# Smaller first projections, a last unit in two halves, and paired port operations in a planned attention kernel

## The chip, the cores and the metric

The kernel runs on one core of a Trainium2 chip. The metric is the device time of one execution in microseconds; less is better. The engines are named as in the profile: PE multiplies matrices (PEld loads its weights), ACT evaluates functions, DVE and POOL work element by element, SP issues DMAs; ACT issues a few DMAs too.

## The reference

Two independent blocks work on inputs of 2048 rows by 512 columns in bf16, and their outputs stand side by side. A is a linear attention, B a full softmax attention, each with 32 heads of 16 columns:

```python
# A: phi(t) = where(t > 0, t + 1, exp(t)) + 1e-6
kv = einsum("bhsd,bhse->bhde", phi(k), v);  z = einsum("bhsd->bhd", phi(k))
o = einsum("bhqd,bhde->bhqe", phi(q), kv) / (einsum("bhqd,bhd->bhq", phi(q), z)[..., None] + 1e-6)
# B: softmax over 2048 keys for 32 heads of 16 columns
p = softmax(einsum("bhqd,bhkd->bhqk", q, k) * 0.25);  o = einsum("bhqk,bhkd->bhqd", p, v)
# each: out = o @ wo
```

## The kernel before, in words

**Work.** Nearly all the work is B's scores: 32 heads x 2048 x 2048. Heads are taken eight at a time (head group `Gp`, four of them), queries 512 at a time (chunk `c`), and even and odd heads apart (`e_`): 32 units `u`. In a unit, four heads lie in four strips of 32 rows of the PE array, `g` = 0 to 3. K^T is kept twice in `KM`, once with the odd heads' rows at zero and once with the even ones', so that a strip of 32 rows yields one head. A block is one head, 128 keys (`j`, 16 of them) and 512 queries: a unit has 64 blocks, the kernel 2048.

**Two ways for a block.** Its score matmul (`qk`, L863) takes 32 rows of `KM` and of `QT`.
- The ACT way: three or two blocks at a time go into the PSUM tiles `pS0` (three banks) and `pS1` (two banks), which alternate, and ACT writes exp of them to `PT` (L1032).
- The D way: the block goes into one of the two banks of `pD`. DVE turns it into 16-bit integers whose bits are nearly those of exp (L944, into `DI`), and POOL adds two constants to these (L968, two blocks at a time, two shifted copies). Three such copies, each with its own scaled V (`VV`), together approximate the exponential.

Then the values are multiplied (L1107), one matmul for an ACT block and three for a D block, 17 columns per head (16 and a column of ones for the denominator), four heads side by side in four column strips, into `pPV`.

**End of a unit** (`unit_done`, L1123 to L1147). DVE transposes `pPV` in 32x32 squares (L1127), takes the reciprocals (L1133), POOL multiplies by them (L1134; DVE does so in the last unit), and after the odd unit DVE transposes back into `ON` (L1139). At the end `pre_job` (L794) multiplies three of the four head blocks of the last 512 rows by `wo` once all scores have been issued, and `last_job` (L805) adds the fourth and copies the result out with DVE or ACT. A copy by DVE is stored by SP, one by ACT by ACT itself (L814).

**A beside it.** A's projections, phi and outputs are jobs of matmuls and DVE operations in the same `pD` banks. `phi_stages` (L687) is an exponential on ACT (L691), a clamp on DVE (L692) and a combination on DVE (L693); `v4_job` (L665) makes `VV` and its two scaled copies (L680). The list of A's jobs is spread over the run by due times between 60 us and `TEND` - 60.

**The order of everything** comes from a planner that runs when the program is built (the loop at L1290). It keeps a clock `T` per engine, candidate operations with ready times and priorities, planned durations (a matmul of 512 columns `MM` = 0.2155, a group of score matmuls `QK` = 0.22, a change of kind of PE work `PH` = 0.11), and picks the earliest, with the priority deciding among those within 0.03 us. `fill_act_cand` (L984) offers the next score group for ACT, `fill_d_cand` (L1040) and `d_pick` a block for D if a `pD` bank is free, DVE's and POOL's backlog is small and no A job is overdue. So the number of blocks on each way is a result of the plan. `POLICY` (L254) has one row of 19 parameters, with a random seed among them, for each 8 us of planned time; the last row serves all later ones. Each engine then runs its own list strictly in the planned order and waits on semaphores where data or buffers ask for it.

**PORT.** The DVE operations of L680, L692 and L693 carry a key `"PORT"`. The planner starts one only when POOL is free and keeps POOL free until it has ended, and the POOL operations read the same key, so the order among them is fixed by semaphores. In the plan a handover costs nothing:

```python
st = max(T[eng], c_[0], T["pool"] if c_[5] else 0.0)          # L1318
...
if c_ is not None and c_[5]:
    T["pool"] = max(T["pool"], st + dur)                       # L1364
```

**The head** (L1150 to L1173) is written by hand. PE runs 28 matmuls on an identity matrix, then transposes the first four tiles of 128 rows of B's x (L562), which DVE and ACT in turn copy to `xTb` (L555). Then PE makes K^T of head group 0 for the first 512 rows (L587, four matmuls of 512 columns into the last bank of `pS1`), DVE writes its even and its odd version (L600), PE makes Q^T (into `pD` bank 0), and ACT copies it (L1166). The planner's clocks start after this, at 10.3 (ACT at 11.2).

## Time and profile before

| | us |
|---|---|
| median of 10 runs | 706.12 (705.59 to 708.21) |
| the profiled execution | 708.2 |
| its span, first to last instruction | 706.4 |
| first exponential starts | 12.21 |
| last exponential ends | 696.23 |
| ACT busy in the span | 686.6 (97%) |
| PE, DVE, POOL busy in the span | 655.9, 560.0, 568.5 |

The span is divided in three: a head before the first exponential, the long middle, and a tail after the last. The profile shows for each group of instructions its line, engine, output and input with their shapes, the count, the busy time, the mean of one in ns, and the idle time of the engine just before them with what ended most of it. An arrow `<-PE pD L863` reads: the wait ended when PE's instruction of L863 on tile pD was done. The number of blocks on each way can be read from the score matmuls: L863 with output pS is counted once for each ACT block, with output pD once for each D block. The granted clock is shown as 9 (90% or more) in all 40 slices; whether PE runs at its full rate is read from the distance of its instructions.

### The profile page before, as it was taken

What the parts mean: (1) busy time and instruction counts of PE and PEld (TensorE: products, weight loads), DVE (VectorE), ACT (ScalarE), POOL (GpSimd) and SP (SyncE); (2) the same over time, 40 slices, a digit from 0 to 9 for tenths busy, and PEclk for the clock granted to TensorE, in tenths of its full rate; (3) what the DMA queues carried; (4) which work ended last, traced back from release to release, by engine and by line L of the source; (5) the groups of instructions that cost most, each with busy time, mean ns of one, the idle gap of its engine ahead of it and who ended that gap; (6) DMA issues with size and microseconds to landing.
All of it is one profiled execution on the core that took longest, in us unless ns stands there. A gap on an engine that the chain in (4) does not pass through costs nothing.

```text
span 706.4 us, 15708 instructions
## 1 busy us (share of the span) xinstructions
PE 655.9 (93%) x6657; PEld 222.0 (31%) x6710; DVE 560.0 (79%) x1000; ACT 686.6 (97%) x642; POOL 568.5 (80%) x343
## 2 busy tenths in 40 slices
PE   8999999999999999999999999999999999999985
PEld 4324443233333333322222233322222222222221
DVE  4778878788788888878888887888888788878772
ACT  4999999999999999999999999999999999999994
POOL 4577666777889887796999879998789988898983
PEclk9999999999999999999999999999999999999999
DMA  9900000000000000010010001000011000101001
GB/s 214 230 4 2 1 2 9 5 12 9 2 2 1 2 1 2 8 39 9 18 38 16 2 1 23 17 21 18 9 31 24 16 1 32 32 31 31 24 9 34
DMA packets 35789, 17.34 MB, mean 25 GB/s; under 512 B 26496, under 2 KB 35200, under 8 KB 35712
## 3 DMA queue, kind: packets, MB, share of 16 engines
q1 hardware_dynamic: 34624, 15.61, 9.3%
q8 instruction: 54, 0.88, 0.5%
q10 hardware_dynamic: 1088, 0.66, 0.3%
q14 instruction: 23, 0.19, 0.1%
HBM read 4.72 MB, written 4.19 MB: 13 GB/s over the span
## 4 chain that ended last, share of the span: by engine, by line
ACT 82%; PE 6%; POOL 6%; DVE 3%; issue 1%; POOLq 0%; DVEq 0%; ACTq 0%
ACT PT L1032 80%; POOL DI L968 6%; ACT EA L691 2%; PE pPV L1107 2%; PE pS L863 2%; DVE DI L944 1%; PE pD L587 1%; PE pD L863 0%; PE pD L1152 0%; DVE KNa L693 0%; PE pD L701 0%; DVE VV L680 0%; PE pS L562 0%; PE pS L587 0%; DVE GR L657 0%
## 5 line engine op out<-in xcount | busy, mean ns | idle before, releaser
L1032 ACT ACTIVATE PT<-pS 128x1536 f16<-128x1536 f32 x587 | 673.8, 1368 | 2.5 <-PE pD L863 1.2
L968 POOL TENSOR_TENSOR DI<-DI,SHC 128x1024 int32<-128x1024 int32 x291 | 544.0, 1888 | 117.5 <-DVE DI L944 52.5
L944 DVE TENSOR_SCALAR DI<-pD 128x512 int16<-128x512 f32 (+1 forms) x572 | 382.5, 692 | 70.3 <-PE pD L863 63.1
L863 PE MATMUL pS<-QT,KM 32*128 32x512 bf16 x1467 | 229.3, 385 | 23.4 <-ACT PT L1032 18.0
L1107 PE MATMUL pPV<-DI,VV 128*17 128x512 f16 x1743 | 243.6, 382 | 1.8 <-POOL DI L968 0.9
L1107 PE MATMUL pPV<-PT,VV 128*17 128x512 f16 x1467 | 241.2, 382 | 1.2 <-ACT PT L1032 1.0
L863 PE MATMUL pD<-QT,KM 32*128 32x512 bf16 x581 | 205.9, 385 | 3.9 <-DVE DI L944 2.7
L863 PEld LDWEIGHTS pS<-QT,KM 32*128 32x128 bf16 x1467 | 56.3, 91 | 221.8 <-ACT PT L1032 180.4
L1107 PEld LDWEIGHTS pPV<-DI,VV 128*17 128x17 bf16 x1743 | 51.4, 88 | 65.6 <-issue 48.0
L1107 PEld LDWEIGHTS pPV<-PT,VV 128*17 128x17 bf16 x1467 | 51.6, 88 | 63.3 <-issue 46.9
L863 PEld LDWEIGHTS pD<-QT,KM 32*128 32x128 bf16 x581 | 49.7, 91 | 49.1 <-DVE DI L944 27.7
L701 PE MATMUL pD<-Wa,xTa 128*128 128x128 bf16 x512 | 36.9, 220 | 0.6 <-DVE DI L944 0.2
L587 PE MATMUL pD<-xTb,Wb 128*128 128x512 bf16 x101 | 29.8, 390 | 4.2 <-issue 2.8
L701 PEld LDWEIGHTS pD<-Wa,xTa 128*128 128x128 bf16 x512 | 28.7, 98 | 13.1 <-DVE DI L944 6.8
L1127 DVE STREAM_TRANSPOSE OT<-pPV 128x512 f32<-128x512 f32 x32 | 22.7, 709 | 8.3 <-PE pPV L1107 8.3
L1134 POOL TENSOR_TENSOR OT<-OT,ZR 128x256 bf16<-128x256 f32 x31 | 19.2, 619 | 7.5 <-DVE KNa L692 3.6
L671 PE MATMUL pD<-Wb,xTb 128*128 128x128 bf16 x256 | 17.8, 220 | 1.0 <-DVE KM L600 0.6
L704 DVE CAST KNa<-pD 128x256 bf16<-128x256 f32 x32 | 13.4, 417 | 6.4 <-PE pD L701 6.1
L782 PE MATMUL pD<-WOa,ONT 128*128 128x512 bf16 x52 | 15.6, 383 | 1.7 <-issue 1.7
L728 PE MATMUL pD<-xTa,Wa 128*128 128x512 bf16 x52 | 15.1, 382 | 1.9 <-issue 1.4
L693 DVE SCALAR_TENSOR_TENSOR KNa<-EA,KNa 128x256 bf16<-128x256 bf16 x32 | 13.4, 420 | 4.1 <-POOL DI L968 3.5
L676 DVE CAST VV<-pD 128x512 bf16<-128x512 f32 x16 | 11.0, 688 | 6.8 <-PE pD L671 6.6
(98 smaller groups left out, 301.3 us busy)
## 6 DMA issues: line engine op xcount, KB each, us to landing
out_dram<-OB SPq DMA_DIRECT2D x16, 128.0 KB, 1.7
out_dram<-KNa SPq DMA_DIRECT2D x14, 128.0 KB, 1.7
Wa<-in_A_wqkv_dram SPq DMA_DIRECT2D x1, 1536.0 KB, 8.3
KM<-KR SPq DMA_DIRECT2D x96, 16.0 KB, 1.8
Wb<-in_B_wqkv_dram SPq DMA_DIRECT2D x2, 384.0 KB, 5.0
Wb<-in_B_wqkv_dram SPq DMA_DIRECT2D x1, 512.0 KB, 4.8
WOa<-in_A_wo_dram SPq DMA_DIRECT2D x1, 512.0 KB, 9.0
VNa<-in_B_wo_dram SPq DMA_DIRECT2D x1, 512.0 KB, 3.7
```

Of the source, the lines that this page charges most:

```text
L587: return e.matmul(f32v(bk), lhsT=Wb[:, cc, kind * 512 + Gp * 128:kind * 512 + Gp * 128 + 128], rhs=xTb[:, cc, sc * 512:(sc + 1) * 512], st ...
L671: return e.matmul(f32v(bk)[:, tl * 128:(tl + 1) * 128], lhsT=xTb[:, cc, t * 128:(t + 1) * 128], rhs=Wb[:, cc, 1024 + Gp * 128:1024 + Gp * ...
L701: return e.matmul(f32v(bk)[:, 128 * x:128 * x + 128], lhsT=xTa[:, cc, (t + i_) * 128:(t + i_ + 1) * 128], rhs=Wa[:, cc, c0:c0 + 128], star ...
L728: return e.matmul(f32v(bk), lhsT=Wa[:, cc, bq * 128:(bq + 1) * 128], rhs=xTa[:, cc, sc * 512:(sc + 1) * 512], start=(cc == 0), stop=(cc == 3))
L782: return e.matmul(f32v(bk), lhsT=src, rhs=WO[:, hb, :], start=(hb == 0), stop=(hb == 3))
L863: return e.matmul(dst, lhsT=KM[32 * g:32 * g + 32, Gp % 2, e_, j * 128:(j + 1) * 128], rhs=QT[32 * g:32 * g + 32, Gp % 2, c * 512:(c + 1) ...
L944: sch.add("dve", lambda e: e.tensor_scalar(DI[:, buf, 0, i * 512:(i + n) * 512], DB[:, bi * 512:(bi + n) * 512], ESC, EB, op0=ALU.mult, op ...
L968: sch.add("pool", lambda e: e.tensor_tensor(DI32[:, buf, 1:3, 0:w], DI32[:, buf, 0, 0:w].unsqueeze(1).broadcast_to([128, 2, w]), SHC32[:]. ...
L1032: sch.add("act", lambda e: e.activation(PT[:, row, c0:c0 + w], SCR[sl][:, 0:w], ACTF.Exp, scale=SC), reads=skeys(sl), writes=[("PT", row, ...
L1107: sch.add("pe", lambda e, g=g, vk=vk, c0=c0, P=P, first=first, last_=last_: e.matmul(PVb[32 * g:32 * g + 17, 0:512], lhsT=VV[:, Gp % 2, vk ...
L1127: sch.add("dve", lambda e: e.transpose(OT[:, 0, :], PVb[:, 0:512]), reads=[("PV", g) for g in range(4)], writes=[("OT", 0)])
L1134: (ml, 0.65 if ml == "pool" else 0.36, f_op(ml, lambda e: e.tensor_tensor(xn[:, :, 16 * e_:16 * e_ + 16], o[:, :, 0:16], zr.unsqueeze(2).b ...
```

## The change

1. **Head.** The first K^T and Q^T are made in halves of 256 columns. On PE the order is: transposes of tiles 0 and 1, K half 0, transposes of tiles 2 and 3, Q half 0, Q half 1, K half 1. DVE writes four masked K pieces of 256 columns instead of two of 512 and copies Q half 1; ACT copies Q half 0. Two K halves lie in the two banks of `pS1`, the Q halves in the two `pD` banks. New keys `KMb` and `QTb` guard the second halves. The planner's clocks start at 7.8 (DVE 8.9, POOL 8.6).
2. **Tail.** The last unit is normalised in two halves of 256 queries (`final_done`), all four steps of one half before the other, all on DVE. `last_job` needs only its half. Its copies are ACT, ACT, DVE, ACT for the four tiles, where they were DVE, ACT, DVE, ACT. Two of the four `pre_job`s may run as soon as no more D blocks are offered (fewer than 12 blocks left).
3. **Pairs.** The two operations L692 and L693 become one planned step, and so do the two L680 of a V job; the instructions stay.
4. **Planner.** A handover of the port is planned: 0.065 from a POOL operation to a PORT operation, 0.17 back. Score groups avoid the row strips of the group just issued; one that shares none may be planned beside it, one that shares one costs 0.09 more. The overflow flag's three matmuls and the denominators' sixteen become parts that other work can come between.
5. **Table.** Nearly all rows of `POLICY` are replaced; there are 86 instead of 87.

```diff
+        def both(*fs):
+            op = lambda bk: [f(bk) for f in fs][-1]
+            op.keys = fs[0].keys
+            return op
+        LKG, LKV = 0.065, 0.17
+        poolop = [False]
+        QQ = 0.09
+        lastq = [(), 0.0]
...
         def flag_job(**kw):
-                ("pe", 1.5, f_pe(mm, k3 + ["identf"])),
+                *halves(mm, k3 + ["identf"], n=3, parts=3, dur=0.45),
...
         def v4_job(t4, Gp, **kw):
-            for k_ in range(2):
-                st.append(("dve", 0.21, f_op("dve", lambda e, k_=k_: e.tensor_scalar(v[k_ + 1], v[0], VSCALE[k_], None, op0=ALU.mult),
-                                             [("VV", r, 0, t4), ("VV1", r)], [("VV", r, k_ + 1, t4), "PORT"])))
+            st.append(("dve", 0.42, both(*[
+                f_op("dve", lambda e, k_=k_: e.tensor_scalar(v[k_ + 1], v[0], VSCALE[k_], None, op0=ALU.mult),
+                     [("VV", r, 0, t4), ("VV1", r)], [("VV", r, k_ + 1, t4), "PORT"]) for k_ in range(2)])))
...
         def phi_stages(n, t_ap, keys):
-                ("dve", 0.067 + n * 0.00026, f_op("dve", lambda e: e.tensor_scalar(...), [], list(keys) + ["PORT"])),
-                ("dve", 0.067 + n * 0.00105, f_op("dve", lambda e: e.scalar_tensor_tensor(...), [("EA", q)], list(keys) + ["PORT"]))]
+                ("dve", 0.134 + n * 0.00131, both(
+                    f_op("dve", lambda e: e.tensor_scalar(...), [], list(keys) + ["PORT"]),
+                    f_op("dve", lambda e: e.scalar_tensor_tensor(...), [("EA", q)], list(keys) + ["PORT"])))]
...
         def take(bl, parts):
+                if u == NU - 1 and left[u] < DEND and "dclosed" not in tok:
+                    tok["dclosed"] = T["pe"]
+                    urgent2.extend(pre_job(tl, "dclosed") for tl in range(2))
...
-                        urgent2.extend(pre_job(tl) for tl in range(4))
+                        urgent2.extend(pre_job(tl, "lastfill") for tl in range(2, 4))
...
         def fill_act_cand():
-            ch = choose(u, n)
+            prev = lastq[0] if pmode[0] == "q" else ()
+            ch = choose(u, n, prev)
...
-            start = max(T["pe"], t0, afree[sl] + LAT, buffree.get(src, 0.0) - 0.5)
-            dur = QK
+            hit = any(g in prev for _, _, g in bl)
+            start = max(lastq[1] + 0.05 if prev and not hit else T["pe"], t0, afree[sl] + LAT, buffree.get(src, 0.0) - 0.5)
+            dur = max(0.03, start + QK - T["pe"]) if start < T["pe"] else QK + (QQ if hit else 0.0)
+            start = max(start, T["pe"])
...
         def fill_d_cand():
-            at = max(T["pe"], min(fr), busy - P["DLEAD"], T["pe"] + d_backlog(T["pe"]) - P["DBL"] + 0.01)
+            prev = tuple(lastq[0]) if pmode[0] == "q" else ()
+            early_ = len(prev) < 4 and bool(prev)
+            at = max(lastq[1] + 0.05 if early_ else T["pe"], min(fr), busy - P["DLEAD"], T["pe"] + d_backlog(T["pe"]) - P["DBL"] + 0.01)
...
+            hit = pk[0][2] in prev
+            dur = max(0.03, at + QK - T["pe"]) if not hit and at < T["pe"] else QK + (QQ if hit else 0.0)
...
+        def final_done(u, t_):
...
+            for h in range(2):
+                w = slice(256 * h, 256 * h + 256)
+                o = OT[:, 0, w].rearrange("p (b r) -> p b r", r=32)
+                xn = XN[:, xb, w].rearrange("p (b r) -> p b r", r=32)
+                zr = ZR[:, 0, 8 * h:8 * h + 8]
+                steps += [
+                    (0.37, False, lambda w=w: sch.add("dve", lambda e: e.transpose(OT[:, 0, w], PVb[:, w]), ...)),
+                    (0.16, False, lambda o=o, zr=zr: sch.add("dve", lambda e: e.reciprocal(zr, o[:, :, 16]), ...)),
+                    (0.22, True, lambda o=o, zr=zr, xn=xn: sch.add("dve", lambda e: e.tensor_tensor(
+                        xn[:, :, 16:32], o[:, :, 0:16], zr.unsqueeze(2).broadcast_to([128, 8, 16]), op=ALU.mult), ...)),
+                    (0.37, False, lambda w=w, h=h: sch.add("dve", lambda e: e.transpose(ON[:, k, w], XN[:, xb, w]), ...))]
+            for tl in range(4):
+                urgent2.append(last_job(tl, ("act", "act", "dve", "act")[tl]))
...
         for t in range(4):
-            now(Job(xT_stages(xsrc, on_keys(t), xTb, "xTb", t, 1, ("dve", "act")[t % 2]), gives=[(1, ("xTb", t))]), SBANKS[t], 7.0)
-        jk = proj_job(0, 0, 1, fast=True)
-        jq = proj_job(0, 0, 0)
...
+            st_ = xT_stages(xsrc, on_keys(t), xTb, "xTb", t, 1, ("dve", "act")[t % 2])
+            for eng, dur, fn in st_:
+                fn(SBANKS[t])
+            tok[("xTb", t)] = 6.0
+            if t == 1:
+                first_proj(SBANKS[4], 1, 0)
+        first_k(SBANKS[4], 0, 0, fk(0))
+        first_proj(DBANK[0], 0, 0)
+        sch.add("act", lambda e: e.activation(QT[:, 0, 0:256], f32v(DBANK[0], 256), ACTF.Copy), ...)
+        first_proj(DBANK[1], 0, 256)
+        sch.add("dve", lambda e: e.tensor_copy(QT[:, 0, 256:512], f32v(DBANK[1], 256)), ...)
+        first_proj(SBANKS[3], 1, 256)
+        first_k(SBANKS[3], 0, 256, [("KMb", 0)])
+        first_k(SBANKS[4], 1, 0, fk(1))
+        first_k(SBANKS[3], 1, 256, [("KMb", 1)])
...
         for k_ in T:
-            T[k_] = 10.3
-        T["act"] = 11.2
-        afree[:] = [10.0, 10.0]
-        jfree[0:2] = [11.4, 10.0]
+            T[k_] = 7.8
+        T["dve"] = 8.9
+        T["pool"] = 8.6
+        afree[:] = [7.6, 8.9]
+        jfree[0:2] = [7.8, 7.8]
...
-                    st = max(T[eng], c_[0], T["pool"] if c_[5] else 0.0)
+                    st = max(T[eng], c_[0], T["pool"] + LKG if c_[5] and poolop[0] else T["pool"] - LKV if c_[5] else 0.0)
...
-                T["pool"] = max(T["pool"], st + dur)
+                T["pool"] = max(T["pool"], st + dur + LKV)
+                poolop[0] = False
+            elif eng == "pool":
+                poolop[0] = True
```

## The prediction, made before the changed kernel was run

> **What bounds the kernel.** I read the shares of busy time first, then one stretch cut out by hand, from the first exponential to the end of the last.
>
> ```profile
> PE 655.9 (93%) x6657; PEld 222.0 (31%) x6710; DVE 560.0 (79%) x1000; ACT 686.6 (97%) x642; POOL 568.5 (80%) x343
> 12.21:696.23 684.02, 642.65 (x6583) 214.58 (x6633) 553.26 (x985) 682.15 (x635) 561.30 (x322) 1.00 0.09 21
> ```
>
> The second line gives busy times in the order PE, PEld, DVE, ACT, POOL. ACT works 682.15 of 684.02 us: inside the stretch it loses 1.87 us. The span of 706.4 us is therefore a head (12.21), ACT's work (682.15), ACT's holes (1.87) and a tail (706.40 - 696.23 = 10.17). The chain of waits agrees: 82% of the span is ACT, 80% the exponentials of L1032. So a gain must shorten the head or the tail, or take blocks away from ACT. The groups of instructions show who else can take them:
>
> ```profile
> L1032 ACT ACTIVATE PT<-pS 128x1536 f16<-128x1536 f32 x587 | 673.8, 1368 | 2.5 <-PE pD L863 1.2
> L968 POOL TENSOR_TENSOR DI<-DI,SHC 128x1024 int32<-128x1024 int32 x291 | 544.0, 1888 | 117.5 <-DVE DI L944 52.5
> L944 DVE TENSOR_SCALAR DI<-pD 128x512 int16<-128x512 f32 (+1 forms) x572 | 382.5, 692 | 70.3 <-PE pD L863 63.1
> ```
>
> Of 2048 score blocks 1467 go through ACT and 581 through DVE and POOL (the counts of score matmuls into pS and pD). The chain shows four exponentials, ten blocks, in 4.52 us, so **a block taken from ACT is worth 0.452 us** (the mean of 1368 ns counts overlap twice). In exchange it costs DVE 0.68 us, POOL 1.888/2 = 0.944 us, and PE two more value matmuls, 2 x 0.2155/4 = 0.11 us. ACT is the bound, but the planner decides how much ACT gets, and this depends on DVE and POOL.
>
> **Part 1, head.** In the timeline:
>
> ```profile
> 5.83 0.60 ACT L555 ACTIVATE xTb<-pS 128x512 bf16<-128x512 bf16 x1 [2.47 <-PE pS L562]
> 6.68 0.60 ACT L555 ACTIVATE xTb<-pS 128x512 bf16<-128x512 bf16 x1 [0.26 <-PE pS L562]
> ...
> 9.26 1.41 DVE L600 TENSOR_SCALAR KM<-pS,PAR 128x512 bf16<-128x512 f32 x2 [2.58 <-PE pS L587]
> ...
> 10.97 0.60 ACT L1166 ACTIVATE QT<-pD 128x512 bf16<-128x512 f32 x1 [3.69 <-PE pD L587]
> 11.77 0.11 PEld L863 LDWEIGHTS pS<-QT,KM 32*128 32x128 bf16 x5 [0.42 <-ACT QT L1166]
> ```
>
> The weight loads of the projections start 0.43 us apart up to 10.72, and 0.21 us afterwards: this head runs at half rate. So a 256-column matmul is 0.214 us and a group of four 0.86. An evacuation starts 0.2 us after the last issue. Estimates for 256 columns: ACT 0.39 us (slope between its 128x1024 and 128x1536 rows), DVE scale 0.46 (the casts: 417 ns for 256, 688 for 512).
> New order, step by step. Transposes of tiles 0 and 1 end at 5.68 (16 x 0.116 from 4.76, half of them); copies as now, the second ends at 6.43. K half 0 waits for it: 6.48 to 7.33. Tiles 2 and 3 stand behind it on PE: 7.33 to 8.26, so their copies end at 8.40 (DVE) and 9.04 (ACT), later than now (6.68, 7.28). Q half 0: 8.26 to 9.12; Q half 1: to 9.97; its DVE copy 10.17 to 10.59; K half 1: to 10.83. The first score matmul then goes at 10.93, behind K half 1, instead of 11.77: **-0.84**. It is not the whole shortening that the 512-column steps suggest, since tiles 2 and 3 lose 1.7 us of their lead. DVE now makes four masked K pieces (K half 1 even, both odd) up to 12.4, and the odd ones hold two banks of the second score tile; so the second score group issues at 12.5 and its exponential at 12.95, while the first ends at 11.37 + 1.34 = 12.71 (1580 ns by its form, less 0.24 of overlap): +0.24. Head: **-0.6**; ends 0 (the gap eaten by a late DVE) and -1.5 (half of the cold matmuls at full rate).
> A rule that speaks here: the Trainium skill, "TensorE: Matmul & The Clock Gate", Part 1, says that the full clock comes after a busy window of about 3.4 us, in a window that runs free of the kernel. The trace agrees as far as it goes: full rate 3.4 to 3.6 us after the stream without holes began at 7.33. By that rule the new stream, which begins at 6.48, would open at 9.9 and K half 1 would be 0.4 us shorter, so the head -1.0 by the page and -0.6 by the rows.
>
> **Part 2, tail.**
>
> ```profile
> 696.71 0.72 DVE L1127 STREAM_TRANSPOSE OT<-pPV 128x512 f32<-128x512 f32 x1 [5.75 <-PE pPV L1107]
> 697.47 0.25 DVE L1133 RECIPROCAL ZR<-OT 128x16 f32<-128x16 f32 x1
> 697.75 0.42 DVE L1134 TENSOR_TENSOR OT<-OT,ZR 128x256 bf16<-128x256 f32 x1
> 698.21 0.71 DVE L1139 STREAM_TRANSPOSE ON<-OT 128x512 bf16<-128x512 bf16 x1
> ...
> 700.73 0.60 ACT L555 ACTIVATE KNa<-pS 128x512 bf16<-128x512 f32 x1 [0.51 <-ACT KNa L555]
> 701.35 1.01 ACTq L814 DMA_DIRECT2D out_dram<-KNa  x1
> ```
>
> Four DVE steps take 2.27 us to the next matmul. A half has the same four at about 0.6 of the time, 0.48 + 0.24 + 0.32 + 0.49 = 1.53, so the first half is ready at 698.24 (0.74 earlier) and the second at 699.71 (0.73 later). The output matmul to ACT's copy takes 0.42 to 0.43. ACT now makes three copies in place of two, and its own store issue holds it: the second copy above stood idle 0.51 us behind the first one's store. So 698.66 + 0.60 + 0.51 + 0.60 + 0.51 + 0.60 = 701.48: the last store issues at 701.50 against 701.35, +0.15. Three stores are under way earlier, which may shorten the last landing (3.4 to 4.6 us here, 1.7 for the stores of the middle): -0.3. I take **0**, with ends -0.8 (ACT's issue hidden) and +0.4. The two pre-products made earlier are 6 x 0.2155 = 1.3 us of PE beside the last exponentials; without that cover the first half would wait 0.5 us for them (they end at 698.72 now).
>
> **Part 3, pairs.** A DVE operation marked PORT and POOL exclude each other in this trace:
>
> ```profile
> 102.93 0.23 DVE L692 TENSOR_SCALAR KNa<-KNa 128x256 bf16<-128x256 bf16 x1
> 103.19 0.30 DVE L680 TENSOR_SCALAR VV<-VV 128x544 bf16<-128x544 bf16 x1
> ...
> 105.49 0.43 DVE L693 SCALAR_TENSOR_TENSOR KNa<-EA,KNa 128x256 bf16<-128x256 bf16 x1 [0.67 <-POOL DI L968]
> 103.57 1.89 POOL L968 TENSOR_TENSOR DI<-DI,SHC 128x1024 int32<-128x1024 int32 x1 [1.14 <-DVE VV L680]
> ```
>
> POOL starts 0.08 us after DVE's L680; DVE's L693, second half of the pair whose first half ran at 102.93, starts 0.03 us after POOL. I followed all 128 such operations (32 L680, 48 L692, 48 L693): they make 103 visits of DVE to the port. POOL's holes at them sum to 89.5 us: 45.5 of the operations (9.6 + 7.0 + 4.5 + 13.4 + 11.0), 103 x 0.115 = 11.8 of handovers, 32.2 of waiting for DVE to come, 0.31 a visit. Paired, there are at most 48 + 16 = 64 visits, 39 fewer. POOL gets back 39 x 0.115 = 4.5 us surely, with the waits 39 x 0.425 = 16.6 us at most: 4.7 to 17.5 blocks. DVE waited 14.3 us for POOL at them; its share of 39 visits with 0.035 each is 6.8 us, 9.9 blocks. The lower end is 0, because POOL also waited 52.5 us for DVE's first pass: POOL isn't always what lacks. I take 7 blocks, between 4.7 and 9.9: 7 x 0.452 = **-3.2**, ends 0 and -7.9. PE's 0.8 us for them lies in its idle 41 us.
> The skill's "SBUF — State Buffer" (A bandwidth-pool intuition that's wrong) has the blocked engine start about 115 ns after DVE's end, where these rows show 80; by the page a visit costs 0.15 and the sure part is 5.9 us instead of 4.5.
>
> **Part 4, the planner.** Counting the handover, overlapping score matmuls of different row groups, the sliced flag and denominator jobs and the new table add no instruction but reorder all of them. They could win ACT's holes (1.87 at most) or open new ones; the nearest rows are ACT's longest waits, 0.5 and 0.7 us. At 0.5 us in one exponential of fifty it is +6. I take 0: PE waited 198 us for ACT at L863 and ACT 2 us for PE, so the score matmuls have slack.
>
> **Sum.** -0.6 + 0 - 3.2 + 0 = -3.8. The profiled execution took 708.2 us, 1.8 outside its span; that is the upper edge of the runs, whose median is 706.12. A difference is carried to the median: **702.3**.
>
> **Rivals.** (a) More converts: all 17 blocks and the holes: 706.1 - 0.6 - 7.9 - 1 = 696.6; for it, POOL idles 19 of 48 us between 12 and 60; against it, the 52.5. (b) The freed port turns into no block, as DVE's wait for pD (63 us) decides: only the head stays, 705.5. (c) Slower: the plan now charges 0.065 + 0.17 = 0.235 us for a handover that it took as free, 64 x 0.235 = 15 us of planned POOL time, 16 blocks. Where planned POOL time decides what is offered, ACT gets them back: 16 x 0.452 = 7.2, less the head 712.7; half of it 709.1. It decides from two pD blocks fewer than 581 (0.6/0.452), by more than 0.2% from five. For it: the rows show 0.115, so the plan overcharges; against it: the pairs save more handovers than are left. (d) The halves bring nothing, because the first exponential still waits for the last K half: then 702.9, inside the forecast.
>
> **Chances.** A measurement of this kernel can tell 0.2%, 1.4 us. Forecast with (d) 0.42, (a) 0.22: faster 0.64. (b) 0.18: same. (c) 0.18: slower. The range leaves out the far ends of (a) and (c): 695.5 to 709.
>
> **What would show it.** pD blocks near 588 and L1032 blocks near 1460; visits to the port near 64; first exponential at 11.4 on a cold clock; last store issue at 701.5 less the gain, with three ACT copies 1.1 apart. Fewer pD blocks than 579, or more than 5 us of holes in ACT, would make it wrong.

## The result, and the profile after

The changed kernel takes 703.55 us in the median of 9 runs (702.07 to 705.50), against 706.33 of the kernel before in 31 runs beside it. The ratio is 0.9957, with a 95% interval from 0.9947 to 0.9967, so 2.8 us or 0.43% are gained. The forecast was 702.3. Its size was near; the sum behind it holds one right term and three wrong ones, which cancel for the most part.

The profiled execution took 703.38 us, with a span of 701.7. The page's first row and its groups, for the changed kernel (L863 is now L871, L944 L956, L968 L980, L1032 L1048, L1107 L1129):

```profile
PE 657.1 (94%) x6688; PEld 225.6 (32%) x6740; DVE 573.0 (82%) x1022; ACT 681.3 (97%) x637; POOL 579.6 (83%) x350
...
L1048 ACT ACTIVATE PT<-pS 128x1536 f16<-128x1536 f32 x581 | 667.8, 1334 | 6.6 <-PE pD L871 4.2
L980 POOL TENSOR_TENSOR DI<-DI,SHC 128x1024 int32<-128x1024 int32 x298 | 555.1, 1888 | 98.0 <-DVE DI L956 45.2
L956 DVE TENSOR_SCALAR DI<-pD 128x512 int16<-128x512 f32 (+1 forms) x588 | 391.6, 691 | 71.9 <-PE pD L871 60.5
...
L871 PE MATMUL pS<-QT,KM 32*128 32x512 bf16 x1453 | 226.4, 385 | 16.2 <-ACT PT L1048 11.6
L871 PE MATMUL pD<-QT,KM 32*128 32x512 bf16 x595 | 212.2, 385 | 5.1 <-DVE DI L956 3.6
```

Read the two last rows first: 1453 blocks now go through ACT and 595 through DVE and POOL, against 1467 and 581. Fourteen blocks moved, twice the seven of the forecast. POOL does 298 additions instead of 291 and waits 45.2 us for DVE's first pass instead of 52.5. But ACT's idle time ahead of its exponentials, 2.5 us before, is 6.6 now.

**The profile of before is a poor measure for the head.** In it the first projections ran at half rate, the first exponential stood at 12.21, and the run took 708.2 us. The head's four matmuls of the first K projection in the timeline of before, and in that of e_tail (below), which has the same head (start, length, engine, line, tiles, count):

```profile
7.33 1.89 PE L587 MATMUL pS<-xTb,Wb 128*128 128x512 bf16 x4 [0.69 <-ACT xTb L555]
```
```profile
6.91 1.04 PE L587 MATMUL pS<-xTb,Wb 128*128 128x512 bf16 x4 [0.69 <-ACT xTb L555]
```

The same four take 1.89 us in one execution and 1.04 in the other, whose first exponential stands at 10.04. The profile of b_warm (below) is before's program with nine small matmuls more in PE's gaps; it began on the full clock too, and its run took 705.79. So the changed kernel is set against b_warm. From the first exponential to the end of the last, b_warm and then the changed kernel (from:to, length, busy PE, PEld, DVE, ACT, POOL):

```profile
9.55:693.80 684.25, 642.59 (x6583) 214.04 (x6633) 553.38 (x985) 682.27 (x635) 561.31 (x322) 1.00 0.09 22
```
```profile
9.76:692.74 682.98, 646.90 (x6611) 219.13 (x6662) 566.66 (x1004) 676.56 (x629) 572.36 (x329) 1.00 0.09 22
```

| us | first exponential | ACT busy in the stretch | ACT's holes in it | tail | span |
|---|---|---|---|---|---|
| b_warm | 9.55 | 682.27 | 1.98 | 10.30 | 704.1 |
| changed kernel | 9.76 | 676.56 | 6.42 | 8.96 | 701.7 |
| difference | +0.2 | **-5.7** | **+4.4** | -1.3 | -2.4 |

So the change took 5.7 us of work from ACT and gave 4.4 back in holes. Nearly all of the holes are five; here are the first three in the timeline of ACT (start, length, engine, line, tiles, and in brackets the idle time before with its releaser):

```profile
18.75 6.97 ACT L1048 ACTIVATE PT<-pS 128x1536 f16<-128x1536 f32 x6 [2.10 <-PE pS L871]
27.23 38.67 ACT L1048 ACTIVATE PT<-pS 128x1536 f16<-128x1536 f32 x34 [1.51 <-PE pD L871]
115.89 0.42 ACT L697 ACTIVATE EA<-KNa 128x256 bf16<-128x256 bf16 x1 [1.19 <-DVE KNa L711]
```

The fourth is 0.80 at 425, the fifth 0.59 at 672. The largest in the profile of before is 0.46. **The first two hardly depend on the chip**: the plan itself has holes of 2.16 and 1.51 us at 14.95 and 23.82 of its own clock. `PT` has six buffers. Six exponentials run from 9.76 to 16.65, and then ACT can't write a seventh, because no value matmul has read one: the first V isn't ready. Its matmuls and cast, in the changed kernel and then in b_warm:

```profile
14.28 0.62 PE L677 MATMUL pD<-Wb,xTb 128*128 128x128 bf16 x8 [0.21 <-DVE DI L956]
15.81 0.69 DVE L682 CAST VV<-pD 128x512 bf16<-128x512 f32 x1 [0.93 <-PE pD L677]
```
```profile
10.69 0.62 PE L671 MATMUL pD<-Wb,xTb 128*128 128x128 bf16 x8 [0.64 <-DVE KM L600]
12.22 0.69 DVE L676 CAST VV<-pD 128x512 bf16<-128x512 f32 x1 [1.00 <-PE pD L671]
```

V comes 3.6 us later: the new plan gives the `pD` banks to D blocks and to the next K projection first (the bracket names DVE's pass L956 as what V's matmuls waited for). Values begin at 17.55 instead of 14.13, and ACT goes on at 18.75. Ahead of the second hole it is the same again: the next V is cast at 24.32 and 25.60, and values begin at 26.03.

The fifth hole stands in the plan too, as 0.78 at 658. **The third and the fourth do not come from the plan**, which has only 0.14 for the third and nothing for the fourth. Ahead of the third, DVE works on the overflow flag. The plan takes each of these one-element operations as 0.1 us; on the chip two of them took 0.87 and 1.81, DVE's next pass waits behind them, PE waits for that pass, and ACT waits for the cast (L711) that comes after it. They carry no `"PORT"` key, and each of the two ends with the POOL addition beside it (at 112.89 and 112.88, at 114.74 and 114.73). In all thirteen profiles such an operation takes 0.14 to 0.16 us or ends within 0.02 us of an addition's end. The longer of the two:

```profile
112.93 1.81 DVE L664 SCALAR_TENSOR_TENSOR GR<-GR 1x1 f32<-1x1 f32 x1
```

At the fourth hole the clock is halved. These are the same 3.41 us in the changed kernel and in a_oldhead (below), which has the same plan (from:to, length, busy PE, PEld, DVE, ACT, POOL, granted clock, DMA):

```profile
422.07:425.48 3.41, 3.24 (x20) 0.95 (x21) 1.77 (x4) 2.61 (x4) 3.41 (x3) 0.50 0.00 0
```
```profile
422.01:425.42 3.41, 3.01 (x34) 1.14 (x31) 2.58 (x4) 3.41 (x5) 3.41 (x3) 1.00 0.00 0
```

At a granted clock of 0.50 ACT loses 0.80 us there, at 1.00 nothing. What sets such a stretch off isn't shown. Of the nine runs of the changed kernel, four list a granted clock of 0.995 and took 703.55 to 705.50 us, and five list 0.998 or 0.999 and took 702.07 to 703.63.

**The tail**, the changed kernel's:

```profile
693.23 0.45 DVE L1158 STREAM_TRANSPOSE OT<-pPV 128x256 f32<-128x256 f32 x1 [5.78 <-PE pPV L1129]
...
695.21 0.60 ACT L563 ACTIVATE KNa<-pD 128x512 bf16<-128x512 f32 x1 [2.47 <-PE pD L814]
696.31 0.60 ACT L563 ACTIVATE KNa<-pD 128x512 bf16<-128x512 f32 x1 [0.51 <-ACT KNa L563]
697.41 0.60 ACT L563 ACTIVATE KNa<-pS 128x512 bf16<-128x512 f32 x1 [0.49 <-ACT KNa L563]
```

The three copies are 1.10 apart, held by their own store issues, as foretold. The last issue stands 5.29 us behind the last exponential (5.12 before); the program ends 3.67 behind that issue (5.05 before, 5.18 in b_warm).

**The port.** Clamp (L699) and combination (L700) now stand together all 48 times; before, a POOL operation ran between them 41 times. All in all DVE visits the port 54 times, against 103; POOL's holes at these visits sum to 84.0 us instead of 98.5 (96.0 in b_warm), counted in the same way in all three traces (the prediction's 89.5 covers the visits it could follow one by one).

### The profile page after: what moved, and what is told of

It is laid out like the page before. It is cut to its first block, busy times and chain, and to the rows that moved or that the text cites. A ratio compares the mean times of both kernels' runs of the same rounds, so it can differ in the third digit from the quotient of the medians.

```text
span 701.7 us, 15790 instructions
## 1 busy us (share of the span) xinstructions
PE 657.1 (94%) x6688; PEld 225.6 (32%) x6740; DVE 573.0 (82%) x1022; ACT 681.3 (97%) x637; POOL 579.6 (83%) x350
## 4 chain that ended last, share of the span: by engine, by line
ACT 80%; PE 11%; DVE 5%; POOL 3%; issue 1%; ACTq 0%; POOLq 0%
ACT PT L1048 77%; PE pPV L1129 4%; PE pS L871 3%; POOL DI L980 2%; ACT EA L697 2%; DVE DI L956 2%; PE pD L871 1%; PE pD L787 1%; PE pD L677 1%; PE pD L708 1%; PE pD L1206 0%; DVE KM L608 0%; DVE VV L686 0%; PE pD L595 0%; DVE KNa L700 0%
## 5 line engine op out<-in xcount | busy, mean ns | idle before, releaser
L1048 ACT ACTIVATE PT<-pS 128x1536 f16<-128x1536 f32 x581 | 667.8, 1334 | 6.6 <-PE pD L871 4.2
L980 POOL TENSOR_TENSOR DI<-DI,SHC 128x1024 int32<-128x1024 int32 x298 | 555.1, 1888 | 98.0 <-DVE DI L956 45.2
L956 DVE TENSOR_SCALAR DI<-pD 128x512 int16<-128x512 f32 (+1 forms) x588 | 391.6, 691 | 71.9 <-PE pD L871 60.5
L1129 PE MATMUL pPV<-DI,VV 128*17 128x512 f16 x1785 | 246.1, 382 | 0.9 <-DVE OT L1184 0.7
L1129 PE MATMUL pPV<-PT,VV 128*17 128x512 f16 x1453 | 242.2, 383 | 1.6 <-ACT PT L1048 1.1
L871 PE MATMUL pS<-QT,KM 32*128 32x512 bf16 x1453 | 226.4, 385 | 16.2 <-ACT PT L1048 11.6
L871 PE MATMUL pD<-QT,KM 32*128 32x512 bf16 x595 | 212.2, 385 | 5.1 <-DVE DI L956 3.6
L871 PEld LDWEIGHTS pS<-QT,KM 32*128 32x128 bf16 x1453 | 55.4, 91 | 193.5 <-ACT PT L1048 145.5
L1129 PEld LDWEIGHTS pPV<-DI,VV 128*17 128x17 bf16 x1785 | 52.4, 88 | 70.7 <-issue 52.2
L871 PEld LDWEIGHTS pD<-QT,KM 32*128 32x128 bf16 x595 | 51.5, 91 | 65.5 <-DVE DI L956 41.4
L1129 PEld LDWEIGHTS pPV<-PT,VV 128*17 128x17 bf16 x1453 | 51.7, 88 | 59.5 <-issue 43.6
L595 PE MATMUL pD<-xTb,Wb 128*128 128x512 bf16 x98 | 28.0, 381 | 4.1 <-issue 2.7
L711 DVE CAST KNa<-pD 128x256 bf16<-128x256 f32 x32 | 13.4, 419 | 6.5 <-PE pD L708 6.5
L677 PEld LDWEIGHTS pD<-Wb,xTb 128*128 128x128 bf16 x256 | 14.5, 98 | 6.9 <-DVE DI L956 3.6
L697 ACT ACTIVATE EA<-KNa 128x256 bf16<-128x256 bf16 x32 | 15.4, 481 | 1.2 <-DVE KNa L711 1.2
```

The source lines that it names most:

```text
L595: return e.matmul(f32v(bk), lhsT=Wb[:, cc, kind * 512 + Gp * 128:kind * 512 + Gp * 128 + 128], rhs=xTb[:, cc, sc * 512:(sc + 1) * 512], st ...
L677: return e.matmul(f32v(bk)[:, tl * 128:(tl + 1) * 128], lhsT=xTb[:, cc, t * 128:(t + 1) * 128], rhs=Wb[:, cc, 1024 + Gp * 128:1024 + Gp * ...
L697: ("act", 0.051 + n * 0.000833, f_op("act", lambda e: e.activation(EA[:, q, 0:n], t_ap, ACTF.Exp), list(keys), [("EA", q)])),
L871: return e.matmul(dst, lhsT=KM[32 * g:32 * g + 32, Gp % 2, e_, j * 128:(j + 1) * 128], rhs=QT[32 * g:32 * g + 32, Gp % 2, c * 512:(c + 1) ...
L956: sch.add("dve", lambda e: e.tensor_scalar(DI[:, buf, 0, i * 512:(i + n) * 512], DB[:, bi * 512:(bi + n) * 512], ESC, EB, op0=ALU.mult, op ...
L980: sch.add("pool", lambda e: e.tensor_tensor(DI32[:, buf, 1:3, 0:w], DI32[:, buf, 0, 0:w].unsqueeze(1).broadcast_to([128, 2, w]), SHC32[:]. ...
```

## The experiments

The kernels fall into two kinds. In six of them (e_..., b_warm, a_...) the planned order of before or of after is held (in e_tail up to the last blocks), and only instructions differ. In the others the planner's rules differ, and then `POLICY` has to be new: its rows are tuned to one exact plan, and with the table kept, any single rule or the new head undone makes the program's own planned end 27 to 40 us later (683.0 otherwise). Each of these got a table from the same kind of search. The planned end is no time of the chip, but it explains why one rule can't be undone by itself.

All results together; ratios are to the runs of before made beside it:

| kernel | ratio, interval | first exp. | ACT busy | holes | tail | D blocks |
|---|---|---|---|---|---|---|
| e_head | 1.0000 [0.9986, 1.0013] | 11.96 | 682.69 | 3.16 | 9.49 | 581 |
| e_tail | 0.9993 [0.9982, 1.0003] | 10.04 | 682.13 | 1.87 | 9.56 | 581 |
| e_pair | 1.0001 [0.9990, 1.0012] | 9.85 | 682.43 | 2.71 | 9.11 | 581 |
| b_warm | 0.9998 [0.9987, 1.0010] | 9.55 | 682.27 | 1.98 | 10.30 | 581 |
| changed kernel | 0.9957 [0.9947, 0.9967] | 9.76 | 676.56 | 6.42 | 8.96 | 595 |
| a_oldhead | 0.9962 [0.9949, 0.9975] | 9.88 | 676.42 | 5.68 | 9.52 | 595 |
| a_sp | 0.9960 [0.9945, 0.9975] | 9.73 | 676.35 | 5.63 | 8.39 | 595 |
| s_full | 0.9980 [0.9967, 0.9994] | 9.71 | 677.59 | 5.51 | 9.49 | 593 |
| s_nopair | 0.9965 [0.9949, 0.9980] | 9.79 | 677.17 | 5.20 | 10.04 | 592 |
| s_before | 0.9995 [0.9983, 1.0008] | 9.71 | 679.03 | 4.89 | 9.47 | 591 |
| s_true | 0.9955 [0.9937, 0.9973] | 9.62 | 676.18 | 6.00 | 8.70 | 597 |
| s_ht | 1.0031 [1.0019, 1.0044] | 11.45 | 679.21 | 9.46 | 10.18 | 590 |

Two things can be seen at once. ACT's work falls with the D blocks, by 0.41 us a block between b_warm and the changed kernel and by 0.32 to 0.46 in the others against b_warm; and every kernel with more D blocks has 4.9 us of holes or more, where before had 1.9. The first exponential of the profiled e_head and s_ht, like before's, stands on the slow clock.

Four of these profiles hold stretches of 3.41 us at a granted clock of 0.50 between the first and the last exponential: the changed kernel one, e_head one, s_full three, s_ht one. Holes in or at these stretches are in the sums of the table: 0.80 in the changed kernel, 1.55 at 259 in e_head (0.28 at the same place in before, which has the same plan), 1.74 at 116 and four smaller ones in s_full (3.2 together), 3.11 at 118 in s_ht.

**e_head, the new head alone.** The head's instructions are the changed kernel's, the planned order is before's:

```diff
-        now(jk, SBANKS[4], 10.5)
-        now(jq, DBANK[0], 11.0)
...
+            if t == 1:
+                first_proj(SBANKS[4], 1, 0)
+        first_k(SBANKS[4], 0, 0, fk(0))
...
+        tok[("Q", 0, 0)] = 11.0
```

> The kernel before with only the new head instructions; the planner's start clocks and ready times are left as they were, so the planned order after the head and the 581 pD blocks stay. Theory (the head is worth its own shortening, and what the changed kernel gave back in the hole of 2.1 us before ACT's seventh exponential comes from its plan, not from the early start): first exponential at 9.8 to 11.4 instead of 12.21, no hole above 0.7 us in ACT before 30 us, time 0.6 to 2.4 us below the kernel before. Rival (an early start only fills the six buffers of PT sooner and then waits for the first V): a hole of 1 us or more at ACT's seventh exponential, time within 0.5 us of the kernel before.

Measured: 706.12, no gain that can be seen. In its profile, whose head ran at half rate, the first exponential stands at 11.96, 0.25 before that of the kernel before at the same rate; and no hole above 0.1 us stands ahead of 30 us, so the rival's reason isn't seen either. The forecast's -0.6 is below what a run tells, but the profiles of other kernels agree: a first exponential at 9.62 to 9.79 with the new head, at 9.55 to 10.04 with the old one, both on the full clock. The new head is worth nothing measurable.

**e_tail, the new tail alone.** The hunks of `pre_job`, `last_job`, `take` and `final_done` in the kernel before:

```diff
-                    push("dve", en + LAT, -1, 0.7, lambda st_, en_: unit_done(u, en_))
+                    if u < NU - 1:
+                        push("dve", en + LAT, -1, 0.7, lambda st_, en_: unit_done(u, en_))
+                    else:
+                        final_done(u, en)
```

> The kernel before with only the new tail; the planned order up to the last blocks and the 581 pD blocks stay. Theory (from the profile of the changed kernel, where the last store issues 5.29 us after the last exponential instead of 5.12, but the span ends 3.67 us after that issue instead of 5.05): about 1.2 us below the kernel before, last issue 0 to 0.3 later after the last exponential, the last store landing more than 1 us sooner after its issue. Rival (the prediction: the landing gives 0.3 and ACT's store issues take it back): within 0.4 us of the kernel before.

Measured: 705.82, 0.4 us below before's 706.18 beside it, with an interval that holds 1. The last issue came 6.14 us behind the last exponential, 1.0 later than in before, and the end 3.42 behind it. The first copy stands 3.31 us behind the last exponential, where the changed kernel has 2.47; the copies are again 1.10 apart. The difference comes from the end of the plan: here value matmuls of two D blocks stand with the last ones behind the last exponential, and DVE's first transpose starts 1.33 us after the exponential's end (0.49 in the changed kernel). The tail gives little and its size depends on what the plan leaves for the end.

**e_pair, the pairs alone.** The first PORT operation of each pair is held back and issued right ahead of the second; the planned order is before's:

```diff
+        def late2(x, f, hl):
+            def op(bk):
+                if x == 0:
+                    hl.append(f)
+                else:
+                    hl.pop(0)(bk)
+                    f(bk)
...
```

> The kernel before with only the pairs: the first of the two PORT operations is issued directly before the second; the plan is left as it was, with its 581 pD blocks. Theory (ACT is the bound, and POOL time given back is worth something only if the planner gives a block to it): visits to the port fall from 103 to about 60, POOL's holes there by 5 to 15 us, the holes of ACT stay below 2.5 us, time within 0.7 us of the kernel before. Rival (fewer handovers shorten the run by themselves): 1.5 us or more below.

Measured: 706.28. The visits fell to 61 and POOL's holes at the port from 98.5 to 90.7 us, but POOL's wait for DVE's first pass grew from 52.5 to 60.1. POOL got 7.8 us at one place and lost 7.6 at the other. Against b_warm, whose head also ran at full rate (96.0 and 50.1), it got 5.3 and lost 10.0. With the order held, no block can move, so this was to be expected; what it shows is that the pairs as such give ACT nothing.

**b_warm, PE kept busy in the old head.** Three more 128-column matmuls on the identity at the start and six behind the transposes:

```diff
-            for i_ in range(28):
+            for i_ in range(31):
...
+        def keep(e):
+            for i_ in range(6):
...
+        sch.add("pe", keep, reads=["identb"], writes=[DBANK[1][3]])
```

> The kernel before with three more matmuls in the first stream of 28 and six small matmuls (128 columns, identity, into an unused pD bank) between the transposes and the first projection, so that PE has no hole from 1.6 us to the first scores; the plan is left as it was. Theory (the distance of the matmuls at the start, 0.43 us for 512 columns up to 10.7 in the kernel before and only up to about 7 in the changed one, is the state of the clock, and a stream without holes opens it sooner): 0.21 us matmuls from 8.5 at the latest, the runs near 708 disappear, median 0.5 to 1.5 us below the kernel before. Rival (the moment is given by something else): same split of runs as before, median within 0.4 us.

Measured: 706.03, no difference in the median. Its 12 runs lie from 704.98 to 707.17 and none near 708, where before beside it has 4 of 35 above 707.8; twelve runs are too few to say that those are gone. So the gaps of the old head aren't shown to decide when the clock opens, and a gain by the new head's denser stream isn't shown.

**a_oldhead, the changed kernel with the old head's instructions**, its planned order and start clocks held:

```diff
-            if t == 1:
-                first_proj(SBANKS[4], 1, 0)
...
+        now(jk, SBANKS[4], 7.0)
+        now(jq, DBANK[0], 7.8)
```

> The changed kernel with the head instructions of the kernel before; the planner's start clocks, the plan and the 595 pD blocks stay as in the changed kernel. Theory (once the clock opens early, both heads start the first exponential within 0.5 us of each other, and the early holes of 2.1 and 1.5 us come from the plan, which holds V back): both holes stay, time within 0.7 us of the changed kernel (about 703.5), so the ratio to the kernel before stays near 0.996. Rival (the halves of the projections are worth 1 us or more): 704.5 or more.

Measured: 703.20, a ratio of 0.9962, beside 0.9957 with the new head. The first hole stays without the new head, and so does the second (1.51):

```profile
18.66 6.05 ACT L1048 ACTIVATE PT<-pS 128x1536 f16<-128x1536 f32 x5 [1.90 <-PE pS L871]
```

So these two holes belong to the plan and not to the new instructions, and the head is worth nothing from this side too.

**a_sp, the first two ACT copies of the tail stored by SP** in the changed kernel:

```diff
-                                      reads=obk(o2), queue="sp" if lane == "dve" else "act", force_signal=True))
+                                      reads=obk(o2), queue="sp" if tl < 3 else "act", force_signal=True))
```

> The changed kernel with the stores of the first two of the last four tiles issued by SP instead of ACT. Theory (ACT's own store issue holds its next copy 0.5 us, and the last copy waits behind two of them): last store issue 0.4 to 0.7 us sooner after the last exponential (5.29 before), time 0.2 to 0.7 below the changed kernel (about 703.0). Rival (the end of the span is set by something after the last landing, or SP's issues queue up): no change, 703.5.

```profile
694.17 1.08 ACT L563 ACTIVATE KNa<-pD 128x512 bf16<-128x512 f32 x2 [2.47 <-PE pD L814]
...
695.76 0.60 ACT L563 ACTIVATE KNa<-pS 128x512 bf16<-128x512 f32 x1 [0.50 <-PE pS L814]
```

Two copies now run as one piece of 1.08 us, with no 0.51 between them; the third waits for its matmul. The last issue stands 4.68 us behind the last exponential instead of 5.29. Its median of 702.45 is the lowest of all, 1.1 below the changed kernel's, but the two ratios overlap widely: the trace shows the 0.6, the runs don't resolve it.

**s_full, s_nopair and s_before** get a new table each, found by the same search of the planner's own planned end: s_full for all rules and instructions of the change, s_nopair for all but the pairs (the slices of the denominators and some of the jobs' priorities are undone with them), s_before for the kernel before as it stands. s_full and s_before differ from their parents in `POLICY` alone, of which one row is shown:

```diff
# s_full against the changed kernel: rows of POLICY
-        (0.15, 3.5, 4.2, 0, 3, 5, 32, 3.0, 1.0, 16, 10.0, 0.0, 0, 0, 633, 1, 0.0, 0.0, 2.0),
+        (0.15, 3.5, 4.2, 0, 3, 4, 32, 3.0, 1.0, 16, 10.0, 0.1, 0, 0, 896, 1, 0.0, 0.0, 2.0),
...
# s_nopair against the changed kernel
-            st.append(("dve", 0.42, both(*[
...
+            for k_ in range(2):
+                st.append(("dve", 0.21, f_op("dve", lambda e, k_=k_: e.tensor_scalar(v[k_ + 1], v[0], VSCALE[k_], None, op0=ALU.mult),
...
-                ("dve", 0.134 + n * 0.00131, both(
+                ("dve", 0.067 + n * 0.00026, f_op("dve", lambda e: e.tensor_scalar(t_ap, t_ap, 0.0, 1e-6, op0=ALU.max, op1=ALU.add), ...)),
```

> The changed kernel with another POLICY table, found by a search of mine segment by segment; all rules and instructions as changed. Its plan gives 593 pD blocks (595 in the changed kernel) and 3.9 us of planned holes in ACT between first and last exponential (5.1). Theory (time = head + ACT's work at 0.40 us for a block moved, measured 5.59/14, + ACT's holes + tail, and the holes are in the plan): 682.15 - 12 x 0.40 + 3.9 = 681.2 from first to last exponential, 1 to 1.8 below the changed kernel's 682.98: time about 702.2. Rival (the table of the change is special, or the holes come from the chip and not from the plan): 703.5 or more.

> The changed kernel without the pairs (each PORT operation is planned by itself, as before; handovers are still charged), with a POLICY table that the same search found for these rules. Its plan gives 592 pD blocks and 5.5 us of holes, and was the best of six searches by 4 us over their mean (690.4 of planned time; with the pairs the mean of six was 686.3). Theory (pairs matter only through what the planner can fit, not by themselves): visits to the port near 100 again, 682.15 - 11 x 0.40 + 5.5 = 683.2 from first to last exponential, time 703 to 704.3, as the changed kernel. Rival (handovers of unpaired operations stall ACT or POOL on the chip beyond the plan): 705 or more.

> The kernel before, all its instructions and rules, with only another POLICY table, found by the same search: 591 pD blocks instead of 581, but 6.1 us of planned holes in ACT. Theory (a block moved counts only if no hole opens): 682.15 - 10 x 0.40 + 6.1 = 684.3 from first to last exponential, time 705.5 to 707, no better than the kernel before. Rival (the table and the blocks it moves are the whole gain, the new rules are not needed): 702 to 703.5.

The stretches of s_nopair and s_before:

```profile
9.79:692.16 682.37, 652.35 (x6652) 215.61 (x6652) 561.27 (x1002) 677.17 (x631) 570.63 (x327) 1.00 0.09 22
```
```profile
9.71:693.63 683.92, 654.71 (x6656) 219.50 (x6654) 557.96 (x998) 679.03 (x631) 569.55 (x327) 1.00 0.09 22
```

Without the pairs the kernel is as fast as the changed one (0.9965, intervals overlap), with 592 D blocks and 68 visits to the port. With the old rules and a fresh table (s_before) no gain over before can be seen (0.9995), though ten blocks moved: ACT works 3.2 us less than in b_warm and its holes grow by 2.9. And s_full, all the rules, came out at 0.9980, with a hole of 1.74 us at 115.76 that isn't in its plan. Ahead of this hole stands the flag's operation again (L664, 1.89 us from 111.71), and from 114.81 to 118.22 the granted clock is 0.50, as it is from 340.09 to 343.50 and from 514.17 to 517.58. All twelve runs of s_full list a granted clock of 0.989 to 0.993, the eight of s_nopair 0.997 or 0.998. So the 0.23% between s_full and the changed kernel, under the same rules, may be the table's or in part the clock's, which isn't shown; it is as large as the effect of a rule, and a ranking of single rules can't be had from one table each.

**s_true and s_ht, the start clocks.** s_true is the changed kernel with start clocks as the chip shows them, a fresh table, and the stores of a_sp; s_ht is the kernel before with the new head, tail and start clocks, a fresh table, and the old planner rules.

```diff
         for k_ in T:
-            T[k_] = 7.8
-        T["dve"] = 8.9
-        T["pool"] = 8.6
-        afree[:] = [7.6, 8.9]
...
+            T[k_] = 9.25
+        T["dve"] = 10.55
+        afree[:] = [9.1, 10.5]
...
```

> The changed kernel with the planner's start clocks set to what the chip showed (first score group at 9.3 instead of 7.8, pS1 free at 10.5, V not before 10.9, when its weights have landed), the first three stores of the last tiles issued by SP, and a table from the same search: 597 pD blocks, 5.3 us of planned holes, none above 0.5 us before 70 us. Theory (the early holes of 2.1 and 1.5 us came from start clocks that promise ACT an earlier start than it gets): no hole above 0.8 us before 60 us, 682.15 - 16 x 0.40 + 5.3 = 681.1 from first to last exponential, tail 8.4, time 701 to 702, below the changed kernel and below it with SP's stores (702.45). Rival (V is late whatever the clocks say): a hole of 1.5 us or more before 30 us, 703 or more.

> The kernel before with the new head and tail and the new start clocks, but with its old planner rules (no pairs, no charged handover, no overlap of score groups, no slices), and a POLICY table of my search for them: 590 pD blocks, 7.1 us of planned holes in ACT, 2.2 of them before the seventh exponential. Theory (a moved block is worth 0.40 us, a hole counts in full, the head nothing, the tail 0.4 to 0.8): 682.15 - 9 x 0.40 + 7.1 = 685.6 from first to last exponential, time 705.8 to 707.3. Rival (head, tail and a fresh table are the gain of the change, the planner's rules are not needed): 702.5 to 704.

```profile
16.81 3.71 ACT L1048 ACTIVATE PT<-pS 128x1536 f16<-128x1536 f32 x3 [0.31 <-PE pD L871]
```
```profile
118.35 1.02 ACT L1047 ACTIVATE PT<-pS 128x1024 f16<-128x1024 f32 x1 [3.11 <-PE pS L874]
```

The first line is the end of the first hole in s_true, the second the largest hole of s_ht. In s_true the first hole falls from 2.10 to 0.31 and the one at 27 is gone, but others open (1.75 at 588, which its plan has as 1.88 at 576, and 0.94 at 132), and the sum of the holes stays at 6.0. Its 702.71 can't be told from the changed kernel's 703.55. So mending the start removes the holes named above and doesn't make the kernel faster by what they cost. In s_ht the holes sum to 9.46 us, and it is slower than before. Of the 3.11 at 118 its plan has 0.93; the flag's operation (L666, 1.88 us from 112.32) stands ahead of it, and the granted clock is 0.50 from 116.86 to 120.27. But its six runs that list a granted clock of 0.997 or 0.998 also lie above before's median of 706.35 (707.41 to 710.35). So head, tail and a new table aren't the gain, and a table can lose with nine more blocks moved.

## Why the prediction was right and where it was wrong

**Right: what bounds the kernel, and how a gain must look.** ACT is busy 99% or more of its stretch in both kernels, and the gain came as blocks taken from ACT. The price of a block was 0.40 us instead of 0.452: 5.6 to 5.7 us over 14 blocks. D blocks (595) went the forecast's way; rival (c), fewer of them because the handover is charged, didn't happen. Rival (b), in which no block moves, didn't happen either, though e_pair shows the mechanism behind it: with the order held, POOL's freed time turns into waiting for DVE.

**Right: the tail at 0.** The issue 5.29 behind the last exponential was foretold at 5.27 (701.50 less 696.23), the first half's matmul at 2.01 and measured at 2.04. (Two halves of 1.53 from 696.71 end at 699.77 and not at the 699.71 given for the second; no term uses it.) The landing is the uncertain term: behind the last issue the old tail ends in 5.05, 4.36, 3.99, 5.18 and 4.14 us (before, e_head, e_pair, b_warm, s_before), the new one in 3.67, 3.42, 4.22, 3.60, 3.85 and 4.89 (the changed kernel, e_tail, a_oldhead, s_full, s_nopair, s_ht): 0.6 less in the mean, 4.5 against 3.9. The issue stands 5.29 to 6.19 behind the last exponential with the new tail (a_sp and s_true aside) and 5.12 to 5.33 with the old one. The -1.3 of the table above is mostly this scatter; e_tail as a whole gave 0.07%.

**Wrong: head, -0.6.** The step that failed is "this head runs at half rate". It was true of that execution and not of the kernel: of thirteen profiles ten ran at full rate by 7 us. There the first exponential stands at 9.55 to 10.04 with the old head (e_tail, e_pair, b_warm, a_oldhead, s_before) and at 9.62 to 9.79 with the new one (the changed kernel, a_sp, s_full, s_nopair, s_true): a difference of 0.1 in the mean. On the slow clock the new head gave 11.96 and 11.45 (e_head, s_ht) where before's profile has 12.21: 0.25 and 0.76 earlier, where 0.6 was forecast. But the slow clock is in three of thirteen profiles only, and e_head and a_oldhead show from both sides that the times don't change. The opening at 9.9 that the prediction reads from the page for the new stream did not come in e_head, where weight loads of 256-column matmuls are still 0.21 us apart at 10.1. The Trainium skill, "TensorE: Matmul & The Clock Gate", Part 1, says that the window in which the clock opens runs free of the kernel, so that the first matmuls vary from run to run; it gives the spread of the transition as 500 ns either way. The runs here vary too, 1.89 against 1.04 us for the same four matmuls, but by more than that: full rate by 7 us or only after 10, and some 2.4 us at the first exponential.

**Wrong in size: pairs, "7 blocks", -3.2.** Fourteen blocks moved, and the pairs aren't shown to be their cause. Counting blocks issued by a given time in b_warm and in the changed kernel, the lead in D blocks is 6 at 60 us, 10 at 150, 8 at 200, 12 at 500 and 14 at the end. The pairs on `phi` run from 69 to 298 and from 318 to 595 us, and 11 of the 48 by 150, so ten of fourteen blocks were ahead when most pairs hadn't run. And s_nopair reaches 592 D blocks and the same time without them, though by its expectation such a table is harder to find: six searches ended at 690.4 of planned time in the mean, with the pairs at 686.3. What the prediction counted is there (visits 103 to 54, POOL's holes at them 14.5 us less), but it is part of a plan that was remade as a whole.

**Wrong: planner, 0.** "PE waited 198 us for ACT at L863 and ACT 2 us for PE, so the score matmuls have slack": this is the step whose failure cost most. An average over the run says nothing of the first 30 us, where the plan filled `PT`'s six buffers before V was there: 3.6 of the 6.42 us of holes. Nor does it tell of the flag's operations (1.19) and the halved clock (0.80), which no term of the sum has. The prediction had put more than 5 us of holes as what would make it wrong, and they came to 6.42. That the total is near the forecast is luck, by cancellation: blocks gave 5.7 instead of 3.2, holes took 4.4 instead of nothing, the head gave nothing.

**Open.** Which of the planner's rules, the handover's charge, the overlap of row strips or the slices, lets the plan give ACT fewer blocks isn't settled. Rules without pairs gave 0.9965 (s_nopair), the old rules with the new head and tail 1.0031 (s_ht), the old rules alone 0.9995 (s_before). That speaks for the rules; but each is one table, and s_full's 0.9980 shows how far a table and the clock that goes with it can miss. Nor did a run show what the chip's time would be with the holes gone and everything else kept.

## What to carry to other kernels

When a plan is remade, count what the bounding engine was given and what it lost as two sums, its busy time and its holes, and follow the lead in blocks over time: it tells in which stretch a gain arose, and so which part of a change can't be its cause. Look in a planner for what its start promises against the chip, since a buffer count with a late producer shows as a hole that stands already in the plan. Before a hole is put down to the plan, look for it in the plan and read the granted clock in it. Before a head is priced from one profile, look at the spacing of its matmuls in several executions.

## What the runs showed that was not expected

- The rate of PE at the start differs between executions of the same head: full rate began by 7 us in ten of thirteen profiles and after 10 in three (before, e_head, s_ht). That moves the first exponential from about 9.8 to 12; the granted clock from 8 to 12 us shows 1.00 in both, so it is the spacing of the matmuls that tells it. Nine small matmuls put into PE's gaps made no measurable difference (0.9998).
- Later in the run, too, the granted clock can fall to 0.50 for 3.41 us in one execution and not in another with the same plan. ACT, waiting for PE, lost 0.80 us in such a stretch in the changed kernel and 1.55 us in e_head.
- The flag's one-element DVE operations, which carry no `"PORT"` key, take 0.15 us alone and up to 1.89 us beside a POOL addition, with whose end they end. The plan takes 0.1, and in the changed kernel a hole of 1.19 us in ACT follows; in before one of them takes 1.68 and no such hole does.
- Behind the last store's issue the end of the program comes 4.0 to 5.2 us later with the old tail's instructions and 3.4 to 4.9 with the new one's.
- POOL's freed time at the port came back as waiting for DVE: -7.8 and +7.6 us in e_pair against before's profile, -5.3 and +10.0 against b_warm's.
